# An earlier first pair, no rounding work or norms at the seam of attention and first product, and last stores on two queues

## The chip, the cores and the metric

The kernel runs on one core of one Trainium2 chip. The metric is device time in microseconds; a kernel's time is the median of its runs. So effects of a few microseconds are read from ratios with their 95% intervals, and from stretches of the trace.

## The reference

```python
# q, k, v: (8, 12, 448, 64); x: (3584, 768); w_in: (768, 2048); w_out: (2048, 768), all float32
q_n, k_n = q / rms(q) * g_q, k / rms(k) * g_k          # over the 64 of a head
attn = softmax(q_n @ k_n^T / 8) @ v                     # per batch and head
x = attn, heads side by side                            # (8*448, 768)
h = maximum(x @ w_in, 0);  out = (h * h) @ w_out
```

## The kernel before

Heads are worked on in pairs (64 + 64 rows of the array), six pairs to a batch, and batches two at a time (a span). The first span's twelve pairs run alone ("first attention"), beside the rounding of the weights: 36 rounds of four **ticks** each, on VectorE, ScalarE and GpSimd, which also form Strassen-like sums of the weights and store them in DRAM. Then comes L1, the first product of span 0 (8 x 7 steps of six matmuls, each step with one weight block from DRAM; one matmul of the program stands as two in a trace), then the second product of one span beside the attention of the next.

What the argument needs (cuts are marked):

```python
ps_o = ctx.enter_context(tc.tile_pool(name="ps_o", bufs=1, space=bass.MemoryType.PSUM))   # one bank "o", one bank "t"
...
def norm(i):                      # pairs of the first attention; later ones: norm_by_squares, same chain
    nc.scalar.activation(sq, raw, AF.Square)
    nc.vector.tensor_reduce(rstd, sq..., AX, ALU.add)
    nc.vector.tensor_scalar(rstd, rstd, 1.0 / D, 1e-6, ALU.mult, ALU.add)
    nc.gpsimd.tensor_tensor(flat, flat, mhalf[:SP, 0:4 * NJ], ALU.pow)
    nc.gpsimd.tensor_tensor(sq[:, 0]..., raw[:, 0]..., rstd..., ALU.mult)
...
def values(i, pe_sums):           # TensorE, into the banks "o" and "t"
    pavs[i] = ps_o.tile([P, S], F32, tag="o", name="pav")
...
def finish(i):                    # VectorE; frees "o" and "t"
    nc.vector.reciprocal(x, tot)
    nc.vector.tensor_tensor(x, pav, x, ALU.mult)
...
def attention_alone():
    for i in range(NAT):          # NAT = 12 pairs
        if i + 3 < NAT:
            load(i + 3)
        scores(i, 0); scores(i, 1)
        if i + 2 < NAT:
            norm(i + 2)
        elif i + 1 == NAT:
            norm(NAT)
            load(NAT + 2)         # goes where pair 12 lay: waits for its norm
        ...
        yield                     # here the loop below does its ticks
        values(i, True)
        finish(i)
...
for u, _ in enumerate(attention_alone()):
    weights(min(8 * (u + 1), 16 + (EARLY - 16) * (u - 1) // (NAT - 2)))      # EARLY = 64 ticks
    if u == NAT - 2:
        load_blocks(5)
...
for u, _ in enumerate(first_product(work, 0)):                               # N1 = 56 steps
    weights(min(ALL, EARLY + (ALL - EARLY) * (u + 1) // (N1 - 5)))
    if u == N1 - 5:
        transposes(NAT)
    if u == N1 - 4:
        norm(NAT + 1)
```

All loads and stores are issued by SyncE, in program order. The score bound (product of the gains) is tested by a branch, and nothing of pair 0 but its load stands ahead of the branch.

## Time and profile before

| | before |
|---|---|
| median of 3 runs | 1463.13 us (1462.04 to 1464.82) |
| profiled span | 1460.2 us |
| TensorE busy / idle | 1417.4 / 42.8 us |
| mean granted clock of TensorE | 0.995 |

The page's first part for the kernel before: busy time, its share of the span and instructions, by engine.

```profile
PE 1417.4 (97%) x4656; PEld 654.3 (45%) x4656; DVE 830.5 (57%) x1156; ACT 451.5 (31%) x650; POOL 560.3 (38%) x363
```

TensorE is the bound, and the other engines cost time only where TensorE waits for them or where such a wait lets its clock fall.

### The profile page before, as it was taken

What the parts mean: (1) busy time and instruction counts of PE and PEld (TensorE: products, weight loads), DVE (VectorE), ACT (ScalarE), POOL (GpSimd) and SP (SyncE); (2) the same over time, 40 slices, a digit from 0 to 9 for tenths busy, and PEclk for the clock granted to TensorE, in tenths of its full rate; (3) what the DMA queues carried; (4) which work ended last, traced back from release to release, by engine and by line L of the source; (5) the groups of instructions that cost most, each with busy time, mean ns of one, the idle gap of its engine ahead of it and who ended that gap; (6) DMA issues with size and microseconds to landing.
All of it is one profiled execution on the core that took longest, in us unless ns stands there. A gap on an engine that the chain in (4) does not pass through costs nothing.

```text
span 1460.2 us, 14323 instructions
## 1 busy us (share of the span) xinstructions
PE 1417.4 (97%) x4656; PEld 654.3 (45%) x4656; DVE 830.5 (57%) x1156; ACT 451.5 (31%) x650; POOL 560.3 (38%) x363
## 2 busy tenths in 40 slices
PE   5998899999999999999999999999999999999997
PEld 2333354444444455444444445544444445555553
DVE  4899799578777623455677633345767753332111
ACT  5887477533232111223232201223323201110000
POOL 3899689643443022533443112443433302221000
PEclk9999899999999999999999999999999999999999
DMA  7686798644444342344344433244445333233443
GB/s 210 183 219 198 231 332 300 212 105 91 93 103 101 81 109 87 99 104 101 88 99 96 110 90 90 87 109 94 96 96 110 77 77 97 87 88 102 106 112 70
DMA packets 423832, 180.38 MB, mean 124 GB/s; under 512 B 275012, under 2 KB 421700, under 8 KB 423748
## 3 DMA queue, kind: packets, MB, share of 16 engines
q1 hardware_dynamic: 423748, 179.37, 46.8%
q8 instruction: 39, 0.64, 0.2%
q14 instruction: 45, 0.37, 0.1%
HBM read 146.28 MB, written 33.03 MB: 123 GB/s over the span
## 4 chain that ended last, share of the span: by engine, by line
PE 84%; DVE 5%; POOL 3%; DMA 3%; issue 2%; ACT 1%; SPq 0%; POOLq 0%; DVEq 0%; ACTq 0%
PE ps L897 32%; PE sc L679 10%; PE pav L703 9%; PE pd L851 9%; PE pc L851 8%; PE pa L851 8%; PE pb L851 4%; PE tot L714 3%; DMA sw<-w1s 1%; POOL gC L500 1%; POOL gC L506 1%; DVE xT L724 1%; DVE acc L692 1%; POOL rstd L627 1%; ACT pr L684 1%
## 5 line engine op out<-in xcount | busy, mean ns | idle before, releaser
L647 POOL TENSOR_TENSOR half<-half,mhalf 128x28 f32<-128x28 f32 x36 | 173.3, 4813 | 346.1 <-DVE half L646 336.0
L897 PE MATMUL ps<-gT,sw 128*128 128x448 f32 x768 | 299.1, 542 | 0.0
L831 POOL TENSOR_TENSOR gT<-gT 128x448 f32<-128x448 f32 x96 | 94.9, 990 | 373.3 <-ACT gT L827 373.3
L897 PE MATMUL ps<-gC,sw 128*128 128x448 f32 x576 | 225.2, 542 | 0.0
L897 PEld LDWEIGHTS ps<-gT,sw 128*128 128x128 f32 x768 | 143.9, 190 | 149.9 <-issue 146.2
L679 PE MATMUL sc<-qkT 64*112 64x448 f32 x768 | 172.2, 568 | 7.0 <-ACT pr L684 4.3
L686 ACT ACTIVATE pr<-sc 112x896 f32<-112x896 f32 x120 | 104.7, 914 | 199.8 <-PE sc L679 199.8
L897 PEld LDWEIGHTS ps<-gC,sw 128*128 128x128 f32 x576 | 108.0, 190 | 112.3 <-issue 111.8
L724 DVE RECIPROCAL xT<-tot 128x448 f32<-128x448 f32 x48 | 141.7, 2952 | 28.6 <-PE tot L714 28.6
L851 PE MATMUL pa<-xT,sw 128*128 128x448 f32 x384 | 154.9, 539 | 0.0
L703 PE MATMUL pav<-pr,vt 112*64 112x448 f32 x672 | 146.1, 549 | 3.2 <-issue 3.2
L827 ACT ACTIVATE gT<-gT 128x448 f32<-128x448 f32 x96 | 55.3, 576 | 288.6 <-DVE gT L866 288.5
L679 PEld LDWEIGHTS sc<-qkT 64*112 64x112 f32 x768 | 61.1, 174 | 105.8 <-issue 73.8
L851 PEld LDWEIGHTS pa<-xT,sw 128*128 128x128 f32 x384 | 72.9, 190 | 71.7 <-issue 71.1
L703 PEld LDWEIGHTS pav<-pr,vt 112*64 112x64 f32 x672 | 44.7, 137 | 91.4 <-issue 79.7
L851 PE MATMUL pd<-xC,sw 128*128 128x448 f32 x192 | 79.4, 550 | 4.0 <-DMA sw<-w1s 3.7
L506 POOL TENSOR_TENSOR gC<-gC 128x384 f32<-128x384 f32 x64 | 80.2, 1271 | 2.5
L851 PE MATMUL pd<-xT,sw 128*128 128x448 f32 x192 | 78.2, 543 | 1.9 <-DVE z L858 1.9
L866 DVE TENSOR_TENSOR gT<-z,pd 128x448 f32<-128x448 f32 x32 | 19.8, 620 | 105.5 <-PE pd L851 105.5
L660 ACT ACTIVATE qkT<-qkT,gains 128x448 f32<-128x448 f32 x36 | 24.1, 669 | 180.0 <-DVE qkT L659 180.0
L851 PE MATMUL pb<-xC,sw 128*128 128x448 f32 x192 | 77.6, 540 | 1.5 <-DVE xC L738 1.5
L851 PE MATMUL pc<-xT,sw 128*128 128x448 f32 x192 | 77.5, 540 | 0.4 <-DMA sw<-w1s 0.4
(94 smaller groups left out, 1618.1 us busy)
## 6 DMA issues: line engine op xcount, KB each, us to landing
sw<-w1s SPq DMA_DIRECT2D x224, 192.0 KB, 2.3
sw<-w2s SPq DMA_DIRECT2D x168, 256.0 KB, 3.3
w1s<-gC SPq DMA_DIRECT2D x8, 1344.0 KB, 7.1
w2s<-gC SPq DMA_DIRECT2D x8, 1344.0 KB, 6.1
out_dram<-osb SPq DMA_DIRECT2D x192, 56.0 KB, 1.8
qk<-in_q_dram SPq DMA_DIRECT2D x144, 56.0 KB, 2.2
qk<-in_k_dram SPq DMA_DIRECT2D x144, 56.0 KB, 2.2
vt<-in_v_dram SPq DMA_DIRECT2D x72, 112.0 KB, 3.2
```

What stands on the lines that cost most here:

```text
L506: nc.gpsimd.tensor_tensor(*[blocks_of(n)[:, i] for i in (dst, x, y)], op)
L647: nc.gpsimd.tensor_tensor(half, half, mhalf, ALU.pow)
L660: nc.scalar.activation(qkT[:, 0, 0], qkT[:, 0, 0], AF.Copy, scale=gains[:, 0:1])
L679: nc.tensor.matmul(sc[:, h, 0:S], qkT[rows, at, 1, c * SP:(c + 1) * SP], qkT[rows, at, 0, :], start=True, stop=True)
L686: nc.scalar.activation(pr, sc[:, :, 0:S], AF.Exp)
L703: nc.tensor.matmul(pavs[i][h * D:(h + 1) * D, :], vs[i][:, h, c, :], pr[:, h, :], start=(c == 0), stop=(c == NJ - 1))
L714: nc.tensor.matmul(tots[i][h * D:(h + 1) * D, :], ones, pr[:, h, :], start=first, stop=last)
L724: nc.vector.reciprocal(x, tot)
L827: nc.scalar.activation(g, src, AF.Relu)
L831: nc.gpsimd.tensor_tensor(g, g, g, ALU.mult)
L851: nc.tensor.matmul(ps, stream[n + i][:, c], rhs[:, c], start=first and c == 0, stop=c == HC - 1, skip_group_check=not first)
L897: nc.tensor.matmul(ps, stream[n][:, c % 4], rhs_of[i][:, c], start=c == 0, stop=c == HF - 1)
```

## The change

Three intents: start TensorE some 6 us earlier, clear the seam between the first attention and L1 of all work that isn't needed there, and halve the issue time of the last stores. What is left out below only moves declarations and changes buffers of the fallback behind the branch, which these inputs don't take.

```diff
 # 1. start: pair 0 is squared, normed, transposed ahead of the branch, q and k apart, pair 1 loaded there too
+def first_pair(tc, q, k, g_q, g_k, held):
+    load_q(nc, qk, q, 0);  bound[0]();  load_k(nc, qk, k, 0)
+    ...                                   # gains, then load_q, load_k of pair 1
+    squares(0);  bound[1]();  squares(1)  # power of 8 columns each, on GpSimd
+    nc.vector.tensor_tensor(sq[:, 0]..., raw[:, 0]..., rstd[:, 0]..., ALU.mult)
+    ...                                   # transposes of k, of q, copies to qkT
 # 2. seam: pair 12's norm, pair 14's load and pair 12's transposes to the end of L1
-            elif i + 1 == NAT:
-                norm(NAT)
-                load(NAT + 2)
...
+        if first == NAT:
+            norm(NAT + 1)                 # in the second attention, before its loop
...
-                if u == N1 - 5:
+                if u == N1 - 4:
+                    norm(NAT)
+                    load(NAT + 2)
+                if u == N1 - 1:
                     transposes(NAT)
-                if u == N1 - 4:
-                    norm(NAT + 1)
 # 3. ticks: first 64 done by attention's step 10 instead of 11; those of L1 two steps later
-                weights(min(8 * (u + 1), 16 + (EARLY - 16) * (u - 1) // (NAT - 2)))
+                weights(min(8 * (u + 1), 16 + (EARLY - 16) * (u - 1) // (NAT - 3), EARLY))
-                weights(min(ALL, EARLY + (ALL - EARLY) * (u + 1) // (N1 - 5)))
+                weights(min(ALL, EARLY + (ALL - EARLY) * (u - 1) // (N1 - 5)))
 # 4. tail: the four stores of the last tile
-                nc.sync.dma_start(rows[...], osb[i:i + 32])
+                queue = queues[i // 32 % len(queues)]     # (nc.sync, nc.scalar) for the last tile
+                queue.dma_start(rows[...], osb[i:i + 32])
```

More of the change, by code (lines that the diff above doesn't have):

```diff
@@ L124, in load @@
         b, h0 = i // NPAIR, 2 * (i % NPAIR)
-        qk = loads.tile([SP, 2, 2, NJ * D], F32, tag="qk", name="qk")
-        vt = loads.tile([SP, 2, NJ, D], F32, tag="vt", name="vt", bufs=3)
+        qk = loads.tile([SP, 2, 2, NJ * D], F32, tag="qk", name="qk", bufs=1)
+        vt = loads.tile([SP, 2, NJ, D], F32, tag="vt", name="vt", bufs=2)
         for dst, src in ((qk[:, 0], q), (qk[:, 1], k), (vt.rearrange("p h j d -> p h (j d)"), v)):
@@ L153, in transposes @@
         qkn = normed.pop(i)
-        qkT = work.tile([P, 2, S], F32, tag="qkT", name="qkT")
+        qkT = work.tile([P, 2, S], F32, tag="qkT", name="qkT", bufs=1)
         for s in range(2):
@@ L308, in places_of, with load_q, load_k @@
     return qk[:, first:second + 1:second - first]
-def load_pair(nc, qk, q, k, i):
+def load_q(nc, qk, q, i):
     _, H, S, D = q.shape
     b, h0 = divmod(2 * i, H)
-    qk = places_of(qk, i, 0)[:S // 4]
-    nc.sync.dma_start(qk[:, 0].rearrange("p (h e) -> p h e", h=2),
+    nc.sync.dma_start(places_of(qk, i, 0)[:S // 4, 0].rearrange("p (h e) -> p h e", h=2),
                       q[b, h0:h0 + 2].rearrange("h (p j) d -> p h (j d)", j=4))
+def load_k(nc, qk, k, i):
+    _, H, S, D = k.shape
+    b, h0 = divmod(2 * i, H)
+    dst = places_of(qk, i, 0)[:S // 4, 1].rearrange("p (j h d) -> p j h d", j=4, h=2)
@@ L319, in load_pair, with squares @@
     for h in range(2):
-        nc.sync.dma_start(qk[:, 1].rearrange("p (j h d) -> p j h d", j=4, h=2)[:, :, h],
-                          k[b, h0 + h].rearrange("(p j) d -> p j d", j=4))
+        nc.sync.dma_start(dst[:, :, h], k[b, h0 + h].rearrange("(p j) d -> p j d", j=4))
+def first_pair(tc, q, k, g_q, g_k, held):
+    nc = tc.nc
+    qk, qkT, ident, mhalf, gains, rstd, bound = held
+    D = q.shape[-1]
+    S = q.shape[2]
+    NJ = 4
+    SP = S // NJ
+    raw, sq = (places_of(qk, 0, n)[:SP] for n in range(2))
+    load_q(nc, qk, q, 0)
+    bound[0]()
+    load_k(nc, qk, k, 0)
+    for i, g in enumerate((g_q, g_k)):
+        for h in range(2):
+            nc.sync.dma_start(gains[h * D:(h + 1) * D, i:i + 1], g.rearrange("(d o) -> d o", o=1))
+    load_q(nc, qk, q, 1)
+    load_k(nc, qk, k, 1)
+    nc.gpsimd.memset(mhalf, -0.5)
+    make_identity(nc, ident)
+    def squares(s):
+        nc.scalar.activation(sq[:, s], raw[:, s], AF.Square)
+        nc.vector.tensor_reduce(rstd[:, s], sq[:, s].rearrange("p (n d) -> p n d", d=D), AX, ALU.add)
+        nc.vector.tensor_scalar(rstd[:, s], rstd[:, s], 1.0 / D, 1e-6, ALU.mult, ALU.add)
+        nc.gpsimd.tensor_tensor(rstd[:, s], rstd[:, s], mhalf[:SP, 0:2 * NJ], ALU.pow)
+    squares(0)
+    bound[1]()
+    squares(1)
+    nc.vector.tensor_tensor(sq[:, 0].rearrange("p (j h d) -> p h j d", j=NJ, h=2),
+                            raw[:, 0].rearrange("p (h j d) -> p h j d", j=NJ, h=2),
+                            rstd[:, 0].rearrange("p (h j) -> p h j ()", h=2).to_broadcast([SP, 2, NJ, D]), ALU.mult)
+    nc.vector.tensor_scalar(gains[:, 0:1], gains[:, 0:1], gains[:, 1:2], float(D) ** -0.5, ALU.mult, ALU.mult)
+    with tc.tile_pool(name="ps_first", bufs=1, space=bass.MemoryType.PSUM) as ps_first:
+        for s, src in ((1, raw[:, 1]), (0, sq[:, 0])):
+            pt = ps_first.tile([2 * D, S], F32, name=f"pt{s}")
+            for j in range(NJ):
+                nc.tensor.transpose(pt[:, j * SP:(j + 1) * SP], src[:, j * 2 * D:(j + 1) * 2 * D], ident[:SP, :SP])
+            if s:
+                nc.scalar.copy(qkT[:, 0, s], pt)
+            else:
+                nc.scalar.activation(qkT[:, 0, s], pt, AF.Copy, scale=gains[:, 0:1])
@@ L335, in attention_then_ffn_bounded @@
     out: bass.AP,
-    qk,
+    held,
 ):
@@ L391, in attention_then_ffn_bounded @@
     ps_m = ctx.enter_context(tc.tile_pool(name="ps_m", bufs=2, space=bass.MemoryType.PSUM))
-    ident = consts.tile([P, P], F32, name="ident")
+    qk, qkT, ident, mhalf, gains, rstd0, _ = held
     ones = consts.tile([SP, D], F32, name="ones")
-    gains = consts.tile([P, 2], F32, name="gains")
-    mhalf = consts.tile([P, 2 * (S // 32)], F32, name="mhalf")
     gT = consts.tile([P, NFC, 2 * S], F32, name="gT")
@@ L400, in attention_then_ffn_bounded @@
     gC = consts.tile([P, 3, HF, S], F32, name="gC")
-    qkT = consts.tile([P, 2, 2, S], F32, name="qkT")
     clamp1 = consts.tile([P, 1], F32, name="clamp1")
@@ L586, in attention_then_ffn_bounded @@
     pts = {}
-    vs, probs, pavs, tots, accs, normed, rstds = {}, {}, {}, {}, {}, {}, {}
+    vs, probs, pavs, tots, accs, normed, rstds = {}, {}, {}, {}, {}, {}, {0: rstd0}
     places = []
@@ L591, in load @@
         if i < NAT:
-            load_pair(nc, qk, q, k, i)
+            load_q(nc, qk, q, i)
+            load_k(nc, qk, k, i)
             return
@@ L882, in second_product, with deliver @@
         done = []
-        def deliver(ct, col, t):
+        def deliver(ct, col, t, queues=(nc.sync,)):
             osb = work.tile([P, S // 32, 32], F32, tag="osb", name="osb")
@@ L887, in deliver @@
             for i in range(0, P, 32):
-                nc.sync.dma_start(rows[2 * span + t, :, :, col * P + i:col * P + i + 32], osb[i:i + 32])
+                queue = queues[i // 32 % len(queues)]
+                queue.dma_start(rows[2 * span + t, :, :, col * P + i:col * P + i + 32], osb[i:i + 32])
         p1s, c11s = {}, {}
@@ L921, in second_product @@
             yield
-        deliver(*done.pop())
+        deliver(*done.pop(), (nc.sync, nc.scalar))
         yield
-    for i, g in enumerate((g_q, g_k)):
-        for h in range(2):
-            nc.sync.dma_start(gains[h * D:(h + 1) * D, i:i + 1], g.rearrange("(d o) -> d o", o=1))
     load_v(0)
-    load(1)
-    nc.gpsimd.memset(mhalf, -0.5)
     nc.vector.memset(clamp1, 1151.0)
@@ L934, in attention_then_ffn_bounded @@
     nc.vector.memset(ones, 1.0)
-    make_identity(nc, ident)
-    norm(0)
-    nc.vector.tensor_scalar(gains[:, 0:1], gains[:, 0:1], gains[:, 1:2], float(D) ** -0.5, ALU.mult, ALU.mult)
     def ahead(u, nxt):
@@ L954, in attention_then_ffn_bounded @@
         norm(1)
-        transposes(0)
-        take_transposes(0)
         with tc.tile_pool(name="first", bufs=2, reuse_waits="tile") as work:
@@ L1012 @@
     nc = tc.nc
-    D = q.shape[-1]
+    S, D = q.shape[-2:]
     bound = ctx.enter_context(tc.tile_pool(name="bound", bufs=1))
@@ L1016, with load_gains, square_of_bound @@
     top = bound.tile([1, 1], F32, name="top")
-    qk = bound.tile([128, 8, 8 * D], F32, name="qk")
-    load_pair(nc, qk, q, k, 0)
-    for i, g in enumerate((g_q, g_k)):
-        nc.sync.dma_start(gg[:, i, :], g.rearrange("(o d) -> o d", o=1))
-    nc.vector.memset(top, 0.0)
-    nc.scalar.activation(top, top, AF.Exp)
-    nc.vector.tensor_tensor(gg[:, 0, :], gg[:, 0, :], gg[:, 1, :], ALU.mult)
-    nc.vector.tensor_tensor(gg[:, 0, :], gg[:, 0, :], gg[:, 0, :], ALU.mult)
-    nc.vector.tensor_reduce(top, gg[:, 0, :], AX, ALU.max)
+    def load_gains():
+        for i, g in enumerate((g_q, g_k)):
+            nc.sync.dma_start(gg[:, i, :], g.rearrange("(o d) -> o d", o=1))
+    def square_of_bound():
+        nc.vector.tensor_tensor(gg[:, 0, :], gg[:, 0, :], gg[:, 1, :], ALU.mult)
+        nc.vector.tensor_tensor(gg[:, 0, :], gg[:, 0, :], gg[:, 0, :], ALU.mult)
+        nc.vector.tensor_reduce(top, gg[:, 0, :], AX, ALU.max)
+    held = (
+        bound.tile([128, 8, 8 * D], F32, name="qk"),
+        bound.tile([128, 2, 2, S], F32, name="qkT"),
+        bound.tile([128, 128], F32, name="ident"),
+        bound.tile([128, 2 * (S // 32)], F32, name="mhalf"),
+        bound.tile([128, 2], F32, name="gains"),
+        bound.tile([S // 4, 2, 8], F32, name="rstd0"),
+        (load_gains, square_of_bound),
+    )
+    with tc.manual_schedule():
+        nc.vector.memset(top, 0.0)
+        nc.scalar.activation(top, top, AF.Exp)
+        first_pair(tc, q, k, g_q, g_k, held)
     bits = nc.values_load(top.bitcast(mybir.dt.int32))
@@ L1032 @@
         with tc.manual_schedule():
-            attention_then_ffn_bounded(tc, *args, qk)
+            attention_then_ffn_bounded(tc, *args, held)
     with small_scores.Else():
```

## The prediction

> **What bounds the kernel now.** I read the page's busy shares first (TensorE busy 1417.4 of 1460.2 us, so only some 43 us are open to any change of order), then TensorE's waits with the idle time and releaser of each, then the timeline around every wait. TensorE's waits up to 300 us:
>
> ```profile
> PE pt L665 <- POOL qk L629: 17.2, 4, 13.1
> PE sc L679 <- ACT pr L684: 4.3, 1, 4.3
> PE pd L851 <- DMA sw<-w1s: 3.7, 1, 3.7
> PE pav L703 <- issue: 3.2, 2, 2.0
> PE pd L851 <- DVE z L858: 1.9, 3, 1.2
> PE pb L851 <- DVE xC L738: 1.5, 1, 1.5
> ```
>
> Columns: microseconds in all, times, longest. From 300 us to the last matmul the same view has a single row of 1.4 us. So the change can only win at three places: the start (first transpose at 13.05), the seam of attention and L1 (140 to 180 us), and the tail (last matmul ends 1452.65, span ends 1460.2). The seam in the timeline, with the idle time ahead in brackets:
>
> ```profile
> 140.08 1.76 PE L679 MATMUL sc<-qkT 64*112 64x448 f32 x8
> 146.16 3.33 PE L679 MATMUL sc<-qkT 64*112 64x448 f32 x8 [4.32 <-ACT pr L684]
> ...
> 166.71 2.52 PE L851 MATMUL pd<-xT,sw 128*128 128x448 f32 x6 [1.20 <-DVE z L858]
> 169.07 2.42 PE L851 MATMUL pa<-xT,sw 128*128 128x448 f32 x6
> 175.19 4.19 PE L851 MATMUL pd<-xC,sw 128*128 128x448 f32 x6 [3.70 <-DMA sw<-w1s]
> ```
>
> The reader is to see that each of the two long waits is followed by slow matmuls: eight scores take 3.33 instead of 1.76 us, six products 4.19 instead of 2.42.
>
> **What the Trainium skill says.** "TensorE: Matmul & The Clock Gate", Part 1, says that after an idle window of about 3.4 us the array's clock falls to half until it has been busy about as long. This trace agrees: the waits of 4.32 and 3.70 us are followed by half-speed matmuls, the one of 1.49 us is not. "DMA: Bandwidth & Descriptors", section "Issuing engines are not separate DMA queues", says that issuing from several engines only saves the sequencer's time; that is the size I give to the two store queues. "GPSIMD Engine Reference", Specifications, says that GpSimd shares its SBUF interface with VectorE; the trace agrees: L533 takes 0.56 us beside an idle GpSimd and up to 1.27 us beside its L500 and L506.
>
> **The start.** Before, nothing but loads and the gain bound runs until 6.1 us; then squares, mean, GpSimd's power (2.92 us for 16 columns), its multiply (1.04), eight cold transposes and two copies come in a row, and scores start at 15.71. The change puts this ahead of the branch with q first. Reworked with the old durations: q (first issue at 0.73) lands at about 3.4; square 0.55, reduce 0.65, power of 8 columns 1.5; k lands near 5.2, its reduce and scalar end about 6.7; q's multiply on VectorE, about 0.7, ends at 7.4; four cold q transposes end at 8.3; the copy waits for the gains (loads issued by 5.7, some 2.3 us to land) and ends at 9.0. Scores at about 9.1, 6.6 us earlier. Pair 1 (loaded before the branch now) then needs square 1.06, reduce and scalar 1.4, power 2.9, multiply 1.0: its transposes move from 20.33 to about 16.3, **4 us**. But not all of it survives. TensorE's next wait (1.13 us, 34.65) hangs on VectorE's finish of pair 0, and that chain goes back to pair 2's k:
>
> ```profile
> 20.33 0.99 PE L665 MATMUL pt<-ident,qk 112*128 112x112 f32 x8 [1.44 <-POOL qk L629]
> ...
> 21.46 1.06 ACT L622 ACTIVATE qk<-qk 112x1024 f32<-112x1024 f32 x1 [1.36 <-DMA qk<-in_k_dram]
> ```
>
> ScalarE does this square, then two exponentials, two copies and the first rounding work; VectorE's reciprocal follows at 30.60. The DMA engines are saturated from 10 to 20 us (share 0.89 and 1.02). Behind the v load stood 2.72 MB (v, pair 1, two weight chunks, pair 2), done at 21.4; now pair 1 is loaded earlier, so 2.26 MB; at the same 250 GB/s it ends about 19.1. So the start is worth **-2.3 us**, bounded by transfers.
>
> **Rounding ticks.** The 64 ticks of the attention are now done by its step 10 (5.33 a step instead of 4.8). From 25 to 95 us VectorE is busy 60.7, ScalarE 62.2 of 70 us, beside TensorE's 66.8; 11% more ticks is about 0.4 us a pair on each. Mostly hidden, but the waits of 1.2 to 1.5 us at 98 and 110 us show that there is little slack: **+1.5 us**.
>
> **The seam.** Removed: the last five ticks, pair 12's norm and pair 14's load with its stop of the store-and-load queue (SyncE's queue waited there for GpSimd and issued weight blocks late). I expect the block wait to go (3.70, and 4.19 - 2.42 = 1.77 of slow clock), the 1.20 for z, and 0.6 of the 1.49 for xC: L738 to L740 run at 0.62 instead of 1.20 to 1.42 us. Sum -7.3. What stays is the 4.32 us at 146: ScalarE's order still has a tick's three instructions (L519, L524, L525 of before) between the copies and the last pair's exponentials, and they wait for VectorE, which runs without a gap from 129.7. Moreover one more L539 (about 1 us) stands ahead of the reciprocal that frees the value bank: +1. Net **-6.3 us**.
>
> **A new wait.** Pair 12's norm moves to step 52 of L1, its transposes to step 55, the last; the scores follow at once. The order of instructions puts its square on ScalarE directly behind the activation of step 52. Before, pair 13's norm stood at exactly this place, so its own rows measure the chain:
>
> ```profile
> 290.02 0.93 ACT L638 ACTIVATE qk<-qk 128x896 f32<-128x896 f32 x1
> ...
> 293.40 4.81 POOL L647 TENSOR_TENSOR half<-half,mhalf 128x28 f32<-128x28 f32 x1 [15.34 <-DVE half L646]
> ...
> 294.94 1.76 PE L679 MATMUL sc<-qkT 64*112 64x448 f32 x8
> ```
>
> Square to end of power takes 293.40 + 4.81 - 290.02 = 8.2 us; then two multiplies (1.97 uncontended, at 156.79) and the second VectorE transpose (0.58), with hand-overs: scores at 290.02 + 11.1 = 301.1, where TensorE has run out at 294.94. That is **6.2 us** of waiting, long enough for the clock to fall, some 2.3 us more (the two cold restarts above cost 1.8 and 2.8): **+8.5 us**.
>
> **The tail.** Four last stores at 0.48 us of issue each, now two and two: **-1.0 us**; the landing stays.
>
> **Sum:** -2.3 + 1.5 - 6.3 + 8.5 - 1.0 = +0.4 us. I lean a little lower, by 1.5 us, since a quarter of a chance stands for the 4.32 us wait and its cold clock (7.1 us) going as well: 1463.1 + 0.4 - 1.5 = **1462.0 us**.
>
> **Rivals.** (1) The seam is cleared fully, the 146 us wait included, and the norm at step 52 finds its way: about 1463 - 2.3 - 14 - 1 = 1446. For it: the change is made for that. Against it: the order of ScalarE and the length of the norm's chain. (2) The earlier ticks make VectorE the bound of the attention, each of nine pairs 0.5 to 1 us longer: 1466 to 1471. For it: VectorE at 87% with rows stretched by GpSimd. Against it: from 53 to 95 us TensorE has no gap at all. (3) The start's gain is hidden wholly by transfers (1464), or shows in full (1460). (4) Pair 14's load, which waits for GpSimd's multiplies of pair 12, holds the queue ahead of the second weight block of L2, and adds 1 to 3 us to the new wait.
>
> **Range and chances.** The terms err by about 1.5 (start), 2 (ticks), 3 (seam), 3 (new wait); together about 5. Range 1454 to 1469. Over 2% would be 29 us, which is most of all the idle time there is, or twice every loss that I found: 1% each.
>
> **What would show it.** Right: first scores at 9 to 10 us, pair 1's transposes near 16, the value wait near 32 still there; a wait of about 4 us for ScalarE's exponential in the last pair; no wait for a weight block within the first ten products; a wait of about 6 us of the first score of pair 12 for ScalarE's or VectorE's qkT, with slow matmuls after it; end of span some 6.6 us after the last matmul instead of 7.5. Wrong: no wait ahead of pair 12's scores, or none at 146; new waits for GpSimd's qk between 30 and 130 us; waits for weight blocks later in L1, since the ticks end two steps later.

## More of the kernel before

One place that the prediction's lines do not show is needed later: VectorE's way to the values of pair 2, in the timeline of the kernel before (start, duration, engine and line, operation, what waited for).

```profile
39.20 0.94 DVE L532 SCALAR_TENSOR_TENSOR gC<-gT,gC 128x768 uint32<-128x768 uint32 x1
...
46.13 0.97 DVE L725 TENSOR_TENSOR xT<-pav,xT 128x448 f32<-128x448 f32 x1
```

The multiply ends at 47.10 and TensorE's next values start at 47.20: they need the bank "o" that this multiply has just read.

## The result, and the profile after

The changed kernel takes **1474.2 us** (1471.2 to 1474.35, 4 runs), beside 1463.97 (1462.04 to 1465.45, 4 runs) for the kernel before. The ratio is 1.0066, with an interval of 1.0047 to 1.0084: 9.7 us slower. Ratios here and below are the mean time of one kernel's runs over that of the other's of the same rounds, so not quite the ratio of the medians. The page's first part for the kernel after:

```profile
PE 1426.6 (97%) x4656; PEld 657.6 (45%) x4656; DVE 837.7 (57%) x1159; ACT 452.1 (31%) x651; POOL 557.8 (38%) x363
```

The same 4656 matmuls take 9.2 us more of TensorE, and its idle time in the span of 1472.5 us is 45.9, only 3.1 us more. The mean granted clock is 0.988 instead of 0.995. So most of the loss appears as **slower matmuls**, not as waiting. TensorE's waits up to 310 us in the kernel after (us in all, times, longest):

```profile
PE pav L749 <- issue: 8.5, 4, 3.1
PE sc L725 <- DVE qkT L705: 5.9, 1, 5.9
PE pt L365 <- DMA qk<-in_k_dram: 5.5, 1, 5.5
PE pt L711 <- POOL qk L675: 4.7, 2, 4.1
...
PE sc L725 <- ACT pr L730: 3.9, 2, 3.4
PE pd L896 <- DVE gT L911: 2.5, 3, 0.9
```

The wait for a weight block (3.7 us before) and the 13.1 us ahead of the first transpose are gone. New are the 5.9 us ahead of pair 12's scores, and the values' waits have grown from 3.2 to 8.5 us. "Issue" there is not an empty instruction queue: each of these waits ends about 0.1 us after VectorE's multiply that reads the bank "o". The view has no releaser for it. TensorE in the timeline after, at the places that the prediction named:

```profile
9.53 3.22 PE L725 MATMUL sc<-qkT 64*112 64x448 f32 x8 [0.77 <-ACT qkT L369]
...
16.84 1.76 PE L711 MATMUL pt<-ident,qk 112*128 112x112 f32 x8 [4.09 <-POOL qk L675]
...
47.18 1.76 PE L749 MATMUL pav<-pr,vt 112*64 112x448 f32 x4 [3.10 <-issue]
...
151.68 2.89 PE L725 MATMUL sc<-qkT 64*112 64x448 f32 x8 [3.40 <-ACT pr L730]
156.12 1.76 PE L749 MATMUL pav<-pr,vt 112*64 112x448 f32 x4 [1.55 <-issue]
...
304.20 3.33 PE L725 MATMUL sc<-qkT 64*112 64x448 f32 x8 [5.94 <-DVE qkT L705]
307.46 4.25 PE L943 MATMUL ps<-gT,sw 128*128 128x448 f32 x8
```

Four values take 0.97 us at full clock and 1.76 in the slow rows; eight scores 1.76, and 3.33 in the slow row at 304.20. The two profiled spans, cut where both kernels do the same thing:

| stretch (starts of TensorE groups) | before | after | change |
|---|---|---|---|
| start of span to scores of pair 3 | 53.4 | 56.5 | +3.1 |
| to scores of the last pair (11) | 86.7 | 90.1 | +3.4 |
| to the first product of L1 | 16.6 | 17.3 | +0.7 |
| to the end of L1 | 138.2 | 134.4 | -3.8 |
| to the third group of pair 12's scores and products | 4.9 | 13.4 | +8.5 |
| to the end of the span | 1160.4 | 1160.9 | +0.5 |

The first row needs care: the program up to there is the same in the kernel before and in its copies with a changed tail, and it still reached pair 3 at 53.4 us in one profile and at 59.3 in another (below). A single profile can thus be off by 6 us there.

### The profile page after: what moved, and what is told of

Read it like the earlier page. It is cut to its first block, busy times and chain, and to the rows that moved or that the text cites. A ratio compares the mean times of both kernels' runs of the same rounds, so it can differ in the third digit from the quotient of the medians.

```text
span 1472.5 us, 14324 instructions
## 1 busy us (share of the span) xinstructions
PE 1426.6 (97%) x4656; PEld 657.6 (45%) x4656; DVE 837.7 (57%) x1159; ACT 452.1 (31%) x651; POOL 557.8 (38%) x363
## 4 chain that ended last, share of the span: by engine, by line
PE 72%; issue 16%; DVE 5%; POOL 5%; SPq 1%; DMA 1%; ACT 1%; POOLq 0%; DVEq 0%; ACTq 0%
PE ps L943 26%; PE pd L896 9%; PE pc L896 8%; PE pa L896 8%; PE pav L749 7%; PE sc L725 6%; PE pb L896 4%; PE tot L760 2%; POOL gC L545 1%; POOL qk L695 1%; POOL gC L551 1%; POOL rstd L673 1%; DVE gC L577 1%; DVE xT L770 1%; DVE gC L561 1%
## 5 line engine op out<-in xcount | busy, mean ns | idle before, releaser
L725 PE MATMUL sc<-qkT 64*112 64x448 f32 x768 | 175.1, 575 | 12.4 <-DVE qkT L705 5.9
L749 PE MATMUL pav<-pr,vt 112*64 112x448 f32 x672 | 149.4, 559 | 8.5 <-issue 8.5
L749 PEld LDWEIGHTS pav<-pr,vt 112*64 112x64 f32 x672 | 45.9, 140 | 99.1 <-issue 86.8
L896 PE MATMUL pc<-xC,sw 128*128 128x448 f32 x192 | 77.5, 539 | 0.0
```

The source lines that it names most:

```text
L725: nc.tensor.matmul(sc[:, h, 0:S], qkT[rows, at, 1, c * SP:(c + 1) * SP], qkT[rows, at, 0, :], start=True, stop=True)
L749: nc.tensor.matmul(pavs[i][h * D:(h + 1) * D, :], vs[i][:, h, c, :], pr[:, h, :], start=(c == 0), stop=(c == NJ - 1))
L896: nc.tensor.matmul(ps, stream[n + i][:, c], rhs[:, c], start=first and c == 0, stop=c == HC - 1, skip_group_check=not first)
```

## The experiments

The theory after reading the traces: the new wait costs 8.5 us as predicted, the denser ticks cost several times their 1.5 us, the start's gain is eaten by VectorE and by the clock, and the relief of the seam is gained once, however many of its causes are removed. (What the runs leave of each part is said below; the part on VectorE did not hold.) The rivals: the start does gain and the ticks cost all the rest; or the lower clock after the waits costs nothing and only the waits do. The letters in what was expected are those of these theories as they stood when each run was sent. Kernels of one group ran on the same chip.

### First group: start, norms, ticks, queues

**e1_start_only**: the kernel before with the new start.

```diff
 kernel before, and:
+        first_pair(tc, q, k, g_q, g_k, held)     # and all that part 1 of the change moves
```

> The kernel before with the new start alone (first pair transposed ahead of the branch, q first); rounding ticks, norms and stores as before. Theory A (the start's gain is lost at the value matmuls of pair 2, which wait for VectorE's finish of pair 1, and the longer wait there lets TensorE's clock fall): first scores near 9.5 us, values of pair 2 at about 47.2 us as before, slow matmuls after them, scores of pair 3 near 56.4 us, total 2 to 4 us slower than before. Rival B (the loss in the attention comes from the faster tick pace alone): no slow matmuls at pair 2, scores of pair 3 near 51.5 us, total 2 us faster than before.

Measured: 1466.81 us, ratio 1.0011 (0.9986 to 1.0037), so +1.6 us instead of the predicted -2.3; the interval reaches from -2.0 to +5.4. The value wait of pair 2 is 3.07 us and is followed by slow matmuls. No gain of the start alone is resolved, though TensorE starts its scores at 9.7 us instead of 15.7.

**e2_norm_early**: the change, with pair 12's norm earlier in L1.

```diff
 kernel after, and:
-                if u == N1 - 4:
+                if u == 7 * (HF - 3):
                     norm(NAT)
+                if u == 7 * (HF - 2):
                     load(NAT + 2)
-                if u == N1 - 1:
+                if u == 7 * (HF - 1):
                     transposes(NAT)
```

> The changed kernel with pair 12's norm at step 35 of L1 instead of 52, pair 14's load at 42 and the transposes at 49 instead of 55. Theory A (the norm's chain ahead of pair 12's scores costs 5.9 us of wait and 2.5 us of fallen clock): no wait ahead of pair 12's scores, 8 us faster than the changed kernel (about 1466). Rival B (the wait only moves, to GpSimd's or the block loads' queue later in L1): less than 4 us.

Measured: 1478.27 us, ratio 1.0089 (1.0064 to 1.0113). The wait ahead of pair 12's scores is gone, and others stand in L1 and once in the second product (4.1 us for a weight block). The timeline of this kernel:

```profile
252.60 4.15 PE L896 MATMUL pd<-xT,sw 128*128 128x448 f32 x6 [3.21 <-DVE z L903]
...
273.56 3.08 PE L896 MATMUL pd<-xT,sw 128*128 128x448 f32 x4 [3.21 <-DMA sw<-w1s]
```

Here the norm is among the ticks of L1; its GpSimd part holds the load, the load holds SyncE's queue (14.0 us of waiting for GpSimd) and the queue holds the weight blocks. So the norm isn't free at this place among the ticks either; other places in L1 were not tried.

**e3_ticks_back**: the change with both old paces of the ticks.

```diff
 kernel after, and:
-    weights(min(8 * (u + 1), 16 + (EARLY - 16) * (u - 1) // (NAT - 3), EARLY))
+    weights(min(8 * (u + 1), 16 + (EARLY - 16) * (u - 1) // (NAT - 2)))
-    weights(min(ALL, EARLY + (ALL - EARLY) * (u - 1) // (N1 - 5)))
+    weights(min(ALL, EARLY + (ALL - EARLY) * (u + 1) // (N1 - 5)))
```

> The changed kernel with the rounding ticks at the pace of before, in the attention and in L1. Theory A (of the 8.3 us lost between pair 2 and pair 11 about 5 come from the wait and the fallen clock at pair 2, which has the same ticks, and 3.3 from the denser ticks of pairs 6 to 9): pair 11 starts about 3 us earlier than in the changed kernel, but about 3 us come back at the seam: total within 2 us of the changed kernel. Rival B (denser ticks cause all of it): pair 11 starts 8 us earlier, total about 5 us faster.

Measured: 1466.52 us, ratio 1.0016 (0.9987 to 1.0045). Within the change the new paces cost 0.0050 of 1464 us, **7.3 us**, give or take some 5 by the two intervals, where 1.5 were predicted. The number is that of rival B, and pair 11 starts 8.1 us earlier than in the change, also as B had it; but 4.8 of these 8.1 us are there at pair 3, ahead of which the ticks are the same in both. From pair 3 to pair 11 the profile gives 86.8 us, the change's 90.1: **3.3 us** for the denser ticks, as theory A had it. L1 is 132.4 us long here, 134.4 in the change, 138.2 before: the seam is as clear with the old ticks as with the new, and the later ticks cost L1 2.0 us.

**e4_queue_only**: the kernel before with the last stores on two queues.

```diff
 kernel before, and:
-        deliver(*done.pop())
+        deliver(*done.pop(), (nc.sync, nc.scalar))     # queues[i // 32 % 2] in deliver
```

> The kernel before with the last stores on two queues and nothing else. Theory A (as the changed kernel's trace has it): from the last matmul to the end of the span 8.0 us instead of 7.55, total +0.5 us. Rival B (the 8.0 was chance; the issue time of two stores is saved): 6.6 us, total -1 us.

Measured: 1467.75 us, ratio 1.0012 (0.9985 to 1.0038): no gain resolved. From the end of the last VectorE transpose to the end of the span this kernel takes 5.34 us; other kernels with two queues 6.70 (after), 5.91, 7.64 and 6.89 (e2, e3, e5), those with one queue 6.21 (before), 6.08, 6.35, 6.40 and 8.29 (e7, e8, e6, e1). This looks like scatter, but it isn't: after, e1, e2, e3 and e5 have the new start, the others the old one, and sorted by start and queues the numbers hardly overlap (table under "The tail" below). This profile also gives the warning above: the program is that of before up to the tail, and yet pair 3 starts at 59.3.

```profile
50.38 1.76 PE L703 MATMUL pav<-pr,vt 112*64 112x448 f32 x4 [3.08 <-issue]
```

The prediction's wait of 2.0 us was one of two states of that place. In nine profiles of kernels with the old start it is 2.0 to 2.2 us (five times, values at 47.2 to 47.7) or 3.05 to 3.08 (four times, values at 50.1 to 50.5).

### Second group: the clock, each norm and tick alone, and the load

**e5_warm**: the change, with filler matmuls in the new wait.

```diff
 kernel after, and:
+            if i == first == NAT:
+                fill = ps_s.tile([SP, 2, 512], F32, tag="s", name="fill")
+                for _ in range(13):
+                    nc.tensor.matmul(fill[:, 0, 0:S], qkT[0:D, 1, 1, 0:SP], qkT[0:D, 1, 0, :], start=True, stop=True)
```

> The changed kernel with 13 filler matmuls (5.5 us, into a spare score tile, results unused) ahead of pair 12's scores, where TensorE waits 5.9 us for the norm. Theory A (the wait lets TensorE's clock fall, which costs 2.5 us after it): the scores start as late as before but take 1.76 us instead of 3.33, and the first products 3.3 instead of 4.25; 2.5 us faster than the changed kernel. Rival B (the slow matmuls after the wait come from something else, such as memory traffic): no change.

Measured in 5 rounds: 1473.42 us (1468.81 to 1476.05), ratio 1.0061 (1.0036 to 1.0085), against 1.0066 of the change. The timeline of this kernel:

```profile
291.78 9.18 PE L827 MATMUL fill<-qkT 64*112 64x448 f32 x24
...
300.90 1.94 PE L725 MATMUL sc<-qkT 64*112 64x448 f32 x7
302.77 3.27 PE L947 MATMUL ps<-gT,sw 128*128 128x448 f32 x8
```

Scores take 1.94 instead of 3.33 and the products 3.27 instead of 4.25: the slow rows were the clock's doing. But my fillers ran 9.2 us, 3.2 longer than the wait (I had allowed 0.42 us each; they took 0.7), so they gave back what they won. The mechanism is shown, the gain is not. The mean also mixes two groups: three runs at a clock of 0.997 or 0.998 took 1468.8 to 1471.0 us, three at 0.991 took 1475.8 to 1476.1, and the profile is one of the first three.

**e6_norms_only**: the kernel before with part 2 of the change alone.

```diff
 kernel before, and:
-                norm(NAT)
-                load(NAT + 2)
...
+                if u == N1 - 4:
+                    norm(NAT)
+                    load(NAT + 2)
+                if u == N1 - 1:
+                    transposes(NAT)
```

> The kernel before with the norms alone moved (pair 12's norm and pair 14's load from the attention's end to step 52 of L1, transposes to 55, pair 13's norm into the next attention). Theory A (the wait of 5.9 us and the fallen clock outweigh the cleared seam, whose wait for a weight block of 3.7 us and its slow clock go): 2 to 5 us slower than before, no wait for a block in the first ten products. Rival B (the seam gives more than the new wait takes): 0 to 4 us faster.

Measured: 1468.06 us, ratio 1.0027 (1.0006 to 1.0047), +3.9. L1 shrinks to 132.8 us (-5.4), and the wait ahead of pair 12's scores is the one that the change has. The timeline of this kernel:

```profile
295.20 3.33 PE L679 MATMUL sc<-qkT 64*112 64x448 f32 x8 [5.94 <-DVE qkT L659]
```

**e7_att_ticks_only**: the kernel before with the denser ticks in the attention alone.

```diff
 kernel before, and:
-    weights(min(8 * (u + 1), 16 + (EARLY - 16) * (u - 1) // (NAT - 2)))
+    weights(min(8 * (u + 1), 16 + (EARLY - 16) * (u - 1) // (NAT - 3), EARLY))
```

> The kernel before with the denser tick pace in the attention alone (64 ticks by step 10, none in step 11). Theory A (one more VectorE instruction ahead of the reciprocal in some pairs makes the value matmuls wait): waits of the values of about 1.7, 2.2 and 1.5 us in pairs 5, 8 and 11 that before does not have, 2 to 5 us slower than before. Rival B (the loss of the changed kernel comes from the ticks in L1 coming later, or from the clock by chance): within 1 us of before.

Measured: 1461.88 us, ratio 0.9982 (0.996 to 1.0004), -2.6, where 2 to 5 us slower was expected; the waits came as expected. It splits in two. TensorE in the timeline of this kernel:

```profile
80.83 0.97 PE L703 MATMUL pav<-pr,vt 112*64 112x448 f32 x4 [1.70 <-issue]
...
115.14 1.69 PE L703 MATMUL pav<-pr,vt 112*64 112x448 f32 x4 [2.22 <-issue]
...
153.50 0.97 PE L703 MATMUL pav<-pr,vt 112*64 112x448 f32 x4 [1.37 <-issue]
```

Ahead of the values of pairs 5, 8 and 11 VectorE now has 8 rounding instructions between one reciprocal and the next, where it had 5, 5 and 7, and TensorE waits for the bank. The last pair starts at 143.9 us instead of 140.1; 0.5 of this is there at pair 3, so the ticks cost 3.4. But no tick is left in step 11, and L1 takes 133.4 us instead of 138.2: this part too clears the seam by itself.

**e8_load_late**: the kernel before with nothing but pair 14's load moved.

```diff
 kernel before, and:
                 norm(NAT)
-                load(NAT + 2)
...
                 if u == N1 - 4:
                     norm(NAT + 1)
+                    load(NAT + 2)
```

> The kernel before with pair 14's load alone moved, from the attention's end to step 52 of L1; norms and ticks as before. Theory A (the queue that stops at this load for GpSimd's norm is what makes the first weight blocks late): no wait for a weight block in the sixth product and no slow matmuls there, 4 to 6 us faster than before. Rival B (the traffic of the rounding makes the blocks late): the wait stays, within 1 us of before.

Measured: **1459.46 us** (1458.24 to 1460.24), ratio 0.9962 (0.9943 to 0.9982): 5.6 us faster than the kernel before, and some 15 faster than the change. SyncE's waits of the kernel before between 150 and 180 us show what went:

```profile
SPq L599 <- POOL qk L649: 8.2, 1, 8.2
```

Line 599 is pair 14's load, which may not overwrite pair 12 before GpSimd has normed it; for 8.2 us nothing behind it, weight blocks included, was issued. TensorE in the timeline of e8:

```profile
173.23 2.52 PE L850 MATMUL pd<-xC,sw 128*128 128x448 f32 x6
```

The product that stood at 4.19 us after 3.70 of waiting takes 2.52 after none, while the wait for z, which I had counted into the seam's gain, stays at 1.20.

### Third group: fillers at other places, two pieces together, L1's ticks

**e9_load_late_fill**: e8 with fillers in the last pair's wait.

```diff
 e8, and:
+            if i + 1 == NAT:
+                fill = ps_m.tile([P, S], F32, tag="m", name="fill")
+                for _ in range(5):
+                    nc.tensor.matmul(fill[0:SP, :], qkT[0:D, 1, 1, 0:SP], qkT[0:D, 1, 0, :], start=True, stop=True)
```

> The kernel before with pair 14's load late (as in e8) and five filler matmuls (3.75 us, results unused) in the wait of 4.3 us of the last pair's third score. Theory A (the clock falls in that wait and costs 2.8 us after it): the scores after it take 1.76 us instead of 3.33 and the first values 0.97 instead of 1.76; 2 to 3 us faster than e8 (about 1457). Rival B (the value matmuls then wait for VectorE's finish of pair 10 instead, which ends when it did): no slow matmuls, but a new wait of about 2 us, within 1 us of e8.

Measured: 1460.95 us, ratio 0.9964 (0.9945 to 0.9984), against 0.9962 of e8: nothing gained. The timeline of this kernel:

```profile
155.46 0.97 PE L703 MATMUL pav<-pr,vt 112*64 112x448 f32 x4 [1.14 <-issue]
...
168.29 1.58 PE L854 MATMUL pb<-xC,sw 128*128 128x448 f32 x2 [2.63 <-DVE xC L738]
```

The fillers run 3.92 us and the clock stays up, and VectorE's work for the values and for xC (2.63 us of wait, 1.73 in e8) takes it back.

**e10_start_fill**: e9 with the new start, and fillers in its two waits.

```diff
 e9 with the new start, and:
+        for _ in range(16):                              # while k loads
+            nc.tensor.matmul(fill, ident[:SP, :SP], ident[:SP, :SP], start=True, stop=True)
...
+            if i == 0:                                   # ahead of pair 1's transposes
+                for _ in range(6):
+                    nc.tensor.matmul(fill[0:SP, :], qkT[0:D, 0, 1, 0:SP], qkT[0:D, 0, 0, :], start=True, stop=True)
```

> As e9, with the changed kernel's start and fillers in it (16 small ones while the first k is loaded, six of 0.75 us ahead of pair 1's transposes, which wait 4 us). Theory A (the start's gain of 6 us at the first scores is eaten by the clock that falls in the wait of 4 us, so with a warm clock it survives): pair 1's scores start near 25.5 us instead of 28.4, 2 to 4 us faster than e9. Rival B (the gain is eaten by VectorE's and ScalarE's chain to pair 2's values, whatever the clock): values of pair 2 at 45 to 47 us, within 1 us of e9.

Measured: 1461.14 us, ratio 0.9961 (0.9939 to 0.9983): the same as e9, so no gain of the start with fillers is resolved either. The timeline of this kernel:

```profile
47.67 1.76 PE L752 MATMUL pav<-pr,vt 112*64 112x448 f32 x4 [3.04 <-issue]
```

Pair 1 is at its transposes 3.2 us earlier than in the kernel before, and pair 2's values 0.5 us later. But e9, on which it builds, has these values at 50.45, and its last pair at 146.2, here 142.2. So the profile shows a gain of 4.0 us up to there that the timed runs don't show; from the last matmul to the end of the span this kernel takes 9.70 us and e9 7.45.

**e11_norms_att_ticks**: e6 and e7 together.

```diff
 e6, and:
+    weights(min(8 * (u + 1), 16 + (EARLY - 16) * (u - 1) // (NAT - 3), EARLY))
```

> The kernel before with two parts together: the norms moved (alone +3.9 us) and the denser ticks of the attention (alone -2.6 us). Theory A (both clear the same waits at the seam, worth some 5.5 us that can be gained once): 6 to 9 us slower than before. Rival B (the parts are independent): +1.3 us.

Measured: 1470.39 us, ratio 1.0042 (1.0014 to 1.0069), +6.1. If each part kept its own effect, the sum would be +3.9 - 2.6 = +1.3; with three intervals of some 3 to 4 us the difference isn't resolved by the times (two of the six runs, at a clock of 0.989, took 1476.5 us, the others 1467.1 to 1472.1). The traces show it: L1 takes 132.3 us, no shorter than with the norms alone (132.8). So the seam is cleared once, and the ticks' 3.4 us in the attention (the last pair starts at 143.7, in e6 at 140.3) are no longer paid for by it.

**e12_l1_ticks_only**: the kernel before with L1's ticks two steps later.

```diff
 kernel before, and:
-    weights(min(ALL, EARLY + (ALL - EARLY) * (u + 1) // (N1 - 5)))
+    weights(min(ALL, EARLY + (ALL - EARLY) * (u - 1) // (N1 - 5)))
```

> The kernel before with the ticks of L1 alone two steps later. Theory A (they pause at the seam's end, but push work later, where VectorE's sums for L1 wait): within 2 us of before, with two or three waits of 0.8 us for gT. Rival B (they are the main loss of the changed kernel): 4 us or more slower.

Measured: 1468.43 us, ratio 1.0020 (0.9999 to 1.0041), +2.9. The first of three such waits in its timeline:

```profile
198.29 2.52 PE L851 MATMUL pd<-xC,sw 128*128 128x448 f32 x6 [0.85 <-DVE gT L866]
```

In all TensorE waits 2.5 us for gT (0.3 before), as in the change. L1 takes 140.3 us, 2.1 more than before. So it isn't free, though the interval just reaches zero.

### Fourth group: is the start a gain or a loss?

**e13_load_late_start**: e8 with the new start.

```diff
 e8, and part 1 of the change
```

> As e8 (the kernel before with pair 14's load late) with the changed kernel's start, no fillers. Theory A (the start keeps about 2 us in equal clock state): 2 us faster than e8, ratio to before near 0.995. Rival B (the gain is eaten at pair 2's values and the longer wait makes the clock fall more often): within 1 us of e8 or slower, ratio 0.996 to 0.998.

Measured: 1461.61 us (1457.02 to 1463.22), ratio 0.9976 (0.9955 to 0.9997).

**e14_old_start**: the change with the old start.

```diff
 kernel after, without part 1 of the change
```

> The changed kernel with the old start alone (norms, both tick paces and two queues as changed). Theory A (the start keeps about 2 us): 2 us slower than the changed kernel. Rival B (it gains nothing, or lets the clock fall more often): as fast, or up to 3 us faster.

Measured: 1470.34 us (1467.61 to 1476.01), ratio 1.0040 (1.0016 to 1.0064).

**e15_after_again**: the change, unaltered, on the same chip.

```diff
 kernel after, no edit
```

> The changed kernel unchanged, for the comparison with e14 on one chip. Both theories: ratio to before near 1.0066.

Measured: 1474.23 us (1473.99 to 1474.49), ratio 1.0065 (1.0047 to 1.0083): the result repeats on another chip.

There are now three pairs of kernels that differ by the start alone (e8 and e13 ran on different chips, each beside its own runs of the kernel before). The columns are: profiled span less TensorE's busy time; TensorE's busy time; mean granted clock of all timed runs (40 runs of before, 4 to 10 of the others); ratio.

| | idle in the profile | busy in the profile | mean clock of the runs | ratio |
|---|---|---|---|---|
| before, then e1 | 42.8, 41.7 | 1417.4, 1422.9 | 0.9945, 0.9912 | 1, 1.0011 |
| e8, then e13 | 40.3, 38.2 | 1417.8, 1418.8 | 0.9962, 0.9937 | 0.9962, 0.9976 |
| e14, then e15 and after | 49.1, 45.8 | 1420.1, 1426.6 | 0.9942, 0.9894 | 1.0040, 1.0065 |

Each time the new start takes 1.1 to 3.3 us of idle time away, and each time TensorE's clock is lower, in the means over several runs too. A clock lower by 0.0025 to 0.0048 over some 1465 us is an estimate of 3.7 to 7.0 us, if all of it falls on matmuls that nothing waits beside. That is an upper bound: part of the lower mean lies at the start itself (from 14 to 26 us the granted clock is 0.72 in after and e1, 1.00 in before and in the other profiles of the table), ahead of the wait for VectorE at pair 2. Within one kernel the clock does go with the time: two runs of e13 at 0.995 and 0.996 took 1457.0 and 1458.8 us, four at 0.991 to 0.994 took 1461.0 to 1463.2; e8's six, at 0.995 to 0.997, took 1458.2 to 1460.2. Where the clock falls can be seen in the last pair of profiles. TensorE in the timeline of e14, at pair 2:

```profile
50.06 0.97 PE L703 MATMUL pav<-pr,vt 112*64 112x448 f32 x4 [3.05 <-issue]
```

And in that of e15:

```profile
46.52 1.76 PE L749 MATMUL pav<-pr,vt 112*64 112x448 f32 x4 [3.05 <-issue]
```

Pair 2's values come 3.5 us earlier in e15 (e14 is in the later of the old start's two states); then the same wait of 3.05 us is followed by slow matmuls in one and by fast ones in the other. From there to pair 3's scores e14 needs 6.2 us and e15 9.0, so of the 3.5 us a single wait takes 2.8.

What tells the two waits apart is where they lie. In all 17 profiles the granted clock changes only in steps of 3.41 us. The view of windows, cut at these steps (length, TensorE's busy time, instructions, granted clock, share of the DMA engines, GB/s), for e14:

```profile
45.10:48.51 3.41, 1.86 (x8) 1.00 0.54 166
48.51:51.92 3.41, 1.86 (x10) 1.00 1.19 282
```

And for e15:

```profile
41.96:45.37 3.41, 1.47 (x8) 1.00 0.70 211
45.37:48.78 3.41, 2.26 (x6) 0.50 1.19 276
```

In e14 the wait lies across a step, 1.55 us of idle time on each side, and the clock stays; in e15 one window holds 1.94 us, and the clock is halved in the next. Over all profiles the clock fell after windows with 1.79 to 3.41 us of idle time, and the most that a window idled without a fall was 1.96 us (e5), so the limit isn't sharp; the windows with the start's fillers in e10 are left out.

## Why the prediction was wrong, point by point

It said 1462.0 us, within 1454 to 1469; it is 1474.2, and the miss to its sum of +0.4 is 9.3 us.

**The start, -2.3 us, predicted as lasting: failed.** The times were right: scores at 9.5 us (9.1 predicted), pair 1's transposes at 16.8 (16.3), pair 1's values 1.9 us earlier. The transfers went as predicted or better: the square of pair 2 starts at 18.1 us instead of 21.5. (By the prediction's own numbers, 0.46 MB less at 250 GB/s are 1.8 us, not 2.3.) Even at pair 3 the mean of seven profiles with the new start and no fillers in it is 53.9 us (51.4 to 56.8), that of nine with the old one 56.0 (53.4 to 59.4), so the predicted size is there. But no timed pair is faster: +1.6, +2 and +3.7 us, each with an interval of 3 us or more to either side. What failed is the step that a gain at pair 3 is a gain at the end. The traces show two things that take it.

First, the end of the program: in every profile the new start comes with a longer way from the last matmul to the end of the span, 1.6 to 2.0 us in the mean (the table under "The tail").

Second, the clock, as the tables above show. A wait of some 3 us lets it fall or not by where it lies across the 3.41 us steps. The new start has the longer wait at pair 2 in five of seven profiles, the old one in four of nine; why, and whether the new start makes falls more frequent or had bad luck, stays open.

VectorE's own way to pair 2's values, in the profile of the kernel after, is no cost of the new start:

```profile
38.38 1.84 DVE L577 SCALAR_TENSOR_TENSOR gC<-gT,gC 128x768 uint32<-128x768 uint32 x1 [0.83 <-ACT gC L570]
...
46.10 0.97 DVE L771 TENSOR_TENSOR xT<-pav,xT 128x448 f32<-128x448 f32 x1
```

It starts L577 0.82 us before its counterpart, after a wait for ScalarE, and runs it at 1.84 us instead of 0.94, so that the multiply ends when it did before. But e14, with the old start, has the same two rows (a wait of 0.88 us, then 1.79 us) and its values at 50.06. These are the two states of this place: like compared with like, pair 2's values come at 45.2 to 45.5 us instead of 47.2 to 47.7, or at 46.5 to 47.5 instead of 50.1 to 50.5. VectorE thus leaves 2 to 3.5 of the 6 us.

**The ticks, +1.5 us: failed.** The step "mostly hidden" took the busy share of VectorE as the measure. What counts is that three pairs get one to three more instructions ahead of the reciprocal: +3.3 to +3.4 us from pair 3 to pair 11 (e7 against before, e11 against e6, the change against e3). The two steps' delay in L1 was not priced at all: it makes L1 2.0 to 2.1 us longer (e3, e12), and e12 is timed at +2.9. Together some 5.4 us by the profiles; e3's timed 7.3, with its uncertainty of 5, also holds the chance of pair 2.

**The seam, -6.3 us: the mechanism right, the size wrong.** From the last pair to the end of L1 the change gains 3.1 us (-3.8 and +0.7 in the table of stretches). The block wait and its slow clock went, for the reason given (SyncE's queue stopped at pair 14's load). The last pair's wait stayed (3.40, about 4 predicted), and the value wait after it was 1.55 (+1 predicted). The wait for xC, of which 0.6 was to go, stayed (1.54, 1.49 before), and the later ticks took 2.0 us of L1 back. For the change itself the lesson is another: norms (with the load), ticks and load alone are three remedies for one wait: L1 shrinks by 5.4, 4.8 and 3.8 us in the profiles of e6, e7 and e8, each alone, and by 5.9 with two of them. The change paid for two remedies and was paid once.

**The new wait, +8.5 us: right.** 5.94 us of waiting (6.2 predicted) for the norm's chain, and 2.55 of slow clock (1.57 in the scores, 0.98 in the products; 2.3 predicted). GpSimd's power stands in the chain with the 4.81 us that it had before. The chain in the timeline of the kernel after:

```profile
296.65 4.81 POOL L693 TENSOR_TENSOR half<-half,mhalf 128x28 f32<-128x28 f32 x1 [11.34 <-DVE half L692]
...
303.41 0.65 DVE L705 STREAM_TRANSPOSE qkT<-qk 128x448 f32<-128x448 f32 x1 [0.25 <-POOL qk L695]
```

**The tail, -1.0 us: right for the queues, and hidden by the start.** From the end of the last matmul to the end of the span, in us:

| | one queue | two queues |
|---|---|---|
| old start | 7.39 to 7.73 (7 profiles) | 6.48 and 6.72 |
| new start | 9.19 to 9.70 (3 profiles) | 7.25 to 8.99 (5 profiles) |

Two queues save about 0.9 us with the old start and 1.3 with the new, as predicted; the new start costs 2.0 us with one queue and 1.6 with two. In the change that makes 8.1 us, where 6.6 was predicted. The stores are not the main reason: from the end of the last transfer the old start takes 2.4 to 2.9 us, the new one 3.0 to 4.9, in the closing drains and semaphores of the program. Why these take longer, no run shows.

**The sum.** By the stretches of the two profiles, with the predicted term in brackets: to pair 3 +3.1 (start, -2.3), to the last pair +3.4 (ticks, +1.5), seam and L1 -3.1 (-6.3), new wait +8.5 (+8.5), rest +0.5 (tail, -1.0). That is +12.4 for +0.4, of 12.3 us between the two spans; the first term is that of two profiles in different states, not the start's worth. The timed difference is 9.7. The timed runs give no second check: the change without the start (e14) +5.9 and the start +3.7 add up by construction, since the 3.7 is the difference of e15 and e14. Of the rivals, the second (VectorE becomes the bound) was right in kind, though in three pairs and not in nine. The fourth came true in the queue alone: SyncE waits 12.6 us there for GpSimd's multiplies of pair 12, and from 310 us on TensorE waits 1.4 us in all.

**The better version.** e8 moves one load and is 5.6 us faster than the kernel before. Neither the new start nor the fillers, added to it, were shown to gain; the two queues, which the profiles show to save about 1 us, and the other parts were not tried on it.

## What to carry to other kernels

When an in-order queue stalls, find the one instruction that stops it and move that alone: several remedies for the same wait gain it once, and each brings its own price. An earlier start of the bound engine lasts only as far as the engine that frees its next buffer gets earlier too; count that engine's instructions ahead of the release, not its busy share. A wait after which the clock falls costs more than itself, and whether it falls can hang on where the wait lies, so judge a change of a few microseconds by the mean clock over many runs as well as by one profile. And before you call a difference of 1 or 2 us scatter, sort the profiles by what their kernels have in common: here the last 7 us held two effects of opposite sign.

## What the Trainium skill lacked or had wrong

- "TensorE: Matmul & The Clock Gate", Part 1, gives an idle window of about 3.4 us, and the prediction used it as a threshold for one wait. The runs show slow values after waits of 2.20 to 2.22 us (1.69 us per four in e7, at 115.14) and fast ones after 3.05 us (0.97 in e14, at 50.06). The page's remark that the window is free-running fits (see e14 and e15 above); its figure as a limit for a single wait does not, and a window need not be idle throughout: 1.94 us of idle time in 3.41 sufficed in e15.
- The same page calls the number of slow matmuls run-variable, but has nothing on what this does to a comparison of two kernels: runs of the kernel before alone differ from 1461 to 1470 us, and with the new start the mean clock of the runs was lower by 0.0025 to 0.0048.
- "GPSIMD Engine Reference", Specifications, says that the SBUF interface is shared with VectorE. The runs agree (VectorE's L577 takes 1.84 us beside GpSimd's multiplies, its counterpart 0.94 beside a power), but I found no page that gives the time of a power on GpSimd, which sets the norm's chain: 2.9 to 4.1 us for 16 columns and 4.81 for 28.
- No page that I found says how a wait for a PSUM bank to be read shows in the view of waits: it is labelled "issue" here, 8.5 us of the kernel after.
